# A 3x3x2 scheme with 15 half products in place of pairs with 11, in the second layer of an attention and two-layer kernel

## The chip, the cores and the metric

The kernel runs on one core of one Trainium2 chip. A core has TensorE (products into PSUM), VectorE (DVE), ScalarE (ACT) and GpSimd (POOL), each with its own instruction stream in program order, and queues for transfers, of which this kernel uses SyncE's (SP). PSUM has eight banks of 128 partitions by 512 f32 columns. The metric is the device time of one execution in microseconds; less is better.

## The reference

Decayed linear attention on 4 x 8 heads of 768 steps, then two layers of two products each on 3072 rows. Only the second layer is touched by the change.

```python
x = _moe_ref(attn_out)              # (3072, 384) -> (3072, 384), rational function between two products
...
def _moe2_ref(x, w_in, w_out) -> np.ndarray:
    h = x @ w_in                    # (3072, 384) @ (384, 2048)
    g = h * np.cos(h)
    return (g @ w_out).astype(np.float32)
```

## The kernel before

Everything is transposed: a layer takes x as 384 rows (three chunks of 128, `NK`) by 3072 columns, six blocks (`NC`) of 512 columns (`TB`), and goes over the 2048 inner rows in 16 steps (`NF`) of 128. One step of one block makes h (128 x 512) as a first product over the three chunks, then g = h cos h on ACT and DVE, then a second product of g into three accumulators in PSUM (`acc`, three banks). To keep f32 accuracy each operand is split into a high and a low part (`hi` rounded to f32r by ACT, `lo` = rest by POOL or DVE), and each product is three passes of TensorE (`PASSES`: hi hi, hi lo, lo hi). So a plain step has 9 matmuls of 512 columns for h and 9 for the second product.

From the second layer's third block on, steps go in pairs (`by_seven`, L486): two steps (two 128-row parts of w_in), two of the three chunks and two column halves of 256 make a 2x2x2 scheme with seven half products, and the third chunk is added plainly. A pair has 11 half products of three passes (`seven`, L573): 21 matmuls of 256 columns and 6 of 512, as both column halves of the third chunk share a weight. The sums of weights (`weights_sums0/1`, L500) and of x (`x_sums0/1`, L533) are made ahead, on DVE and POOL; the sums of products are made by ACT copies out of PSUM and POOL additions (`seven_out0/1`, `seven_sums`), and added into h's bank by DVE (`seven_add`, L624).

The order on each engine is written by hand (`manual_schedule`), step by step in `layers(n)` (L813): first product of step n (`gemm1`), ACT and DVE work of the steps before (`rational`, `cosine`), second product of the step 4 or 5 before (`lag`, `second`), then loads, splits and conversions of weights. The first layer has n from 0 to 95 (`N1` = 96), the second from 96 to 191; block 2 of the second begins at n = 128. Weights come as f64 words and are converted by ACT and DVE (`to_f32`, `tick`), split by `w_hi` and `w_lo`; those of the second layer's w_in go to DRAM (`wd`) and come back by `w_load`, those of w_out stay in SBUF (`ws[1]`, tiles `w1_0` to `w1_15`). Finished accumulators are copied out by `acc_out` (L668), the middle one by DVE, the other two by ACT.

h's banks in pairs: `h_bank` (L495) gives b1, b2, r1, b0 in turn; r0 takes the products that are copied out.

Of the kernel before, what the change touches and what calls it, by code (L numbers as in the profile page):

```python
# [19 lines left out]
HP = 4  # L20
# [19 lines left out]
def attn_then_two_moe(ctx, tc, kqT, aT, vP, w1i, w1o, ma, mb, w2i, w2o, out):  # L40
# [6 lines left out]
    wd = dram.tile([NF + NO, 128, 2, DM], F32, name="wd")  # L47
# [37 lines left out]
    in_p = main.enter_context(tc.tile_pool(name="in", bufs=3))  # L85
# [27 lines left out]
    ws = [[wp.tile([128, 2, DM], F32R, name=f"w{s}_{i}") for i in range(NF)] for s in range(2)]  # L113
# [38 lines left out]
    def words_bank(w):  # L152

        if slot[0] < LEAD:
            return words_t
        if N1 + 3 < slot[0] - LEAD < N1 + 2 * NF - 1:
            return bank(f"r{w[2] % 2}", (128, TB), I32)[:, :DM]
        return None
# [31 lines left out]
    def w_lo(engs):  # L190
        engs = list(engs)
        while to_lo:
            (m, s, i), hi = to_lo.pop(0)
            at = early(m, s, i)
            lo = ws[s][i][:, 1] if at is None else v_t[at % 3][:, :DM].bitcast(F32R)
            engs[0].tensor_tensor(
                out=lo, in0=stage.pop((m, s, i)), in1=hi.bitcast(F32), op=ALU.subtract
            )
            engs.append(engs.pop(0))
            ready.add((m, s, i))  # L200
            if at is not None:
                nc.sync.dma_start(out=wd[at, :, 0], in_=hi.bitcast(F32))
                nc.sync.dma_start(out=wd[at, :, 1], in_=lo.bitcast(F32))
# [254 lines left out]
    N1 = NC * NF  # L458
# [23 lines left out]
    s_in = {}  # L482
    x_t = {}
    held = {}

    def by_seven(n):  # L486

        m, blk, f = where(n)
        return m == 1 and 1 < blk and (blk < NC - 1 or f < NF - 2)

    def lag(n):

        return 5 if n < N1 or by_seven(n) else 4

    def h_bank(n):  # L495
        if n < N1 + 2 * NF:
            return bank(f"b{n % 3}")
        return bank((("b1", "b2"), ("r1", "b0"))[n % 2][n // 2 % 2])

    def weights_sums0(j):  # L500

        a = temp("z", shape=(128, 4, 128))
        for i in range(2):
            w = ws[0][2 * j + i].bitcast(F32)
            nc.vector.tensor_tensor(
                out=a[:, 2 * i:2 * i + 2].rearrange("p a b -> p (a b)"), in0=w[:, 0, 0:256], in1=w[:, 1, 0:256], op=ALU.add
            )
        held["sums"] = t = temp("g", shape=(128, 4, 128))
        nc.gpsimd.tensor_tensor(out=t[:, 0], in0=a[:, 2], in1=a[:, 3], op=ALU.add)
        nc.gpsimd.tensor_tensor(out=t[:, 1], in0=t[:, 0], in1=a[:, 0], op=ALU.subtract)  # L510
        nc.gpsimd.tensor_tensor(out=t[:, 2], in0=a[:, 0], in1=a[:, 2], op=ALU.subtract)
        nc.gpsimd.tensor_tensor(out=t[:, 3], in0=a[:, 1], in1=t[:, 1], op=ALU.subtract)

    def weights_sums1(j):

        if j == 0:
            held["kq"] = const.tile([128, 5 * 2 * HP * C], F32R, tag="kq", name="s_in")
            held["s1"] = [const.tile([128, 128], F32R, tag=f"s{i}", name=f"s1_{i}") for i in range(2)]
        if j < 6:
            flat = held["kq"][:, 2 * DM * j:2 * DM * (j + 1)].rearrange("p (a b c) -> p a b c", a=2, b=3)  # L520
            s = [flat[:, i] for i in range(2)]
        else:
            s = [
                const.tile([128, 3, 128], F32R, tag=f"v{2 * (j - 6) + i}", name=f"s_in{j}{i}") for i in range(2)
            ]
        first = held["s1"] if j == NF // 2 - 1 else [ws[0][2 * j + 1][:, i, 0:128] for i in range(2)]
        t = held.pop("sums")
        for hi, lo, of in ((first[0], first[1], t[:, 0]), (s[0], s[1], t[:, 1:])):
            nc.scalar.activation(out=hi, in_=of, func=AF.Copy)
            nc.gpsimd.tensor_tensor(out=lo, in0=of, in1=hi.bitcast(F32), op=ALU.subtract)  # L530
        s_in[j] = [[first[i]] + [s[i][:, k] for k in range(3)] for i in range(2)]

    def x_sums0(blk):  # L533

        raw = xt[1, blk][:, 1].bitcast(F32)
        t = [in_p.tile([128, TB], F32, tag="p", name="t") for _ in range(2)]
        nc.vector.tensor_tensor(
            out=t[0].rearrange("p (a b) -> p a b", a=2), in0=raw[:, 0:2, HT:],
            in1=raw[:, 0].rearrange("p (a b) -> p a b", a=2), op=ALU.subtract,
        )  # L540
        nc.vector.tensor_tensor(out=t[1][:, :HT], in0=raw[:, 1, HT:], in1=t[0][:, :HT], op=ALU.subtract)
        nc.vector.tensor_tensor(out=t[1][:, HT:], in0=raw[:, 1, :HT], in1=t[1][:, :HT], op=ALU.subtract)
        held["t"] = t

    def x_sums1(blk):

        t = held.pop("t")
        tag, words = (("st", 4 * DM), ("a", 3 * HP * (C + 1)))[blk % 2]
        to = const.tile([128, words], F32R, tag=tag, name=f"x_t{blk}")[:, :6 * HT].rearrange(
            "p (a b c) -> p a b c", a=2, b=3  # L550
        )
        if blk < NC - 1:
            first = [xt[1, blk][:, i, 0, HT:] for i in range(2)]
        else:
            first = [held["kq"][:, 12 * DM + HT * i:12 * DM + HT * (i + 1)] for i in range(2)]
        x_t[blk] = [[first[i]] + [to[:, i, k] for k in range(3)] for i in range(2)]
        for hi, lo, of in (
            (first[0], first[1], t[0][:, :HT]), (to[:, 0, 0], to[:, 1, 0], t[0][:, HT:]),
            (to[:, 0, 1:], to[:, 1, 1:], t[1].rearrange("p (a b) -> p a b", a=2)),
        ):  # L560
            nc.scalar.activation(out=hi, in_=of, func=AF.Copy)
            nc.vector.tensor_tensor(out=lo, in0=of, in1=hi.bitcast(F32), op=ALU.subtract)

    def products(out, parts):

        left = sum(len(p) for p in parts)
        first = True
        for a, b, cs in parts:
            for w, xx in PASSES:
                nc.tensor.matmul(out[:, cs], a[w], b[xx], start=first, stop=True, skip_group_check=True)  # L570
                first = False

    def seven(n, which):  # L573

        _, blk, f = where(n)
        j = f // 2
        x, t, s = xt[1, blk], x_t[blk], s_in[j]
        e, o = ([[ws[0][2 * j + i][:, w, k * 128:(k + 1) * 128] for w in range(2)] for k in range(NK)] for i in range(2))
        left, right, both = slice(0, HT), slice(HT, TB), slice(0, TB)

        def part(k, cs):
            return [x[:, i, k, cs] for i in range(2)]

        def sums(of, k):
            return [of[i][k] for i in range(2)]

        if which == 0:
            y = bank("r0")
            products(y, ((sums(s, 1), sums(t, 2), left), (e[0], part(0, left), right)))
            T[n] = {"m": y}  # L590
        elif which == 1:
            y = bank("r0")
            products(y, ((sums(s, 0), sums(t, 0), left), (sums(s, 2), sums(t, 1), right)))
            T[n]["m"] = y
        else:
            he, ho = h_bank(n - 1), h_bank(n)
            products(he, ((e[2], part(2, both), both), (e[1], part(1, left), left), (sums(s, 3), part(1, right), right)))
            products(ho, ((o[2], part(2, both), both), (o[1], sums(t, 3), left)))
            T[n - 1]["h"] = he
            T[n] = {"h": ho, "of": T[n - 1]}  # L600

    def seven_out0(n):

        d = T[n]
        d["q"] = raw_p.tile([128, 3, HT], F32, tag="raw", name="q")
        nc.scalar.activation(out=d["q"][:, 0:2].rearrange("p a b -> p (a b)"), in_=d["m"], func=AF.Copy)
        nc.gpsimd.tensor_tensor(out=d["q"][:, 0], in0=d["q"][:, 0], in1=d["q"][:, 1], op=ALU.add)

    def seven_out1(n):
        d = T[n]  # L610
        d["p"] = temp("z", shape=(128, 2, HT))
        nc.scalar.activation(out=d["p"].rearrange("p a b -> p (a b)"), in_=d["m"], func=AF.Copy)

    def seven_sums(n):

        d = T[n]
        q, p = d["q"], d["p"]
        nc.gpsimd.tensor_tensor(out=q[:, 2], in0=q[:, 0], in1=p[:, 0], op=ALU.add)
        d["o"] = temp("g", shape=(128, 2, HT))
        nc.gpsimd.tensor_tensor(  # L620
            out=d["o"], in0=q[:, 0:3:2], in1=p[:, 1:2].to_broadcast([128, 2, HT]), op=ALU.add
        )

    def seven_add(n):  # L624

        d = T[n]
# [496 lines left out]
```

## Time and profile before

| | us |
|---|---|
| three timed executions | 939.75, 944.48, 943.57 (median 943.57) |
| profiled execution | 940.65 |
| its span, first to last instruction | 938.8 |
| TensorE busy | 906.9 |
| DVE, ACT, POOL busy | 713.1, 688.8, 723.7 |
| first product by pairs, from its first matmul | 661.40 on |
| last matmul ends | 932.7 |

The profile names an instruction group by its line, engine, operation and tiles (out<-in). Busy matmul intervals overlap each other, since a matmul is recorded until its last result; how often one can begin is read from the starts of the next. The granted TensorE clock is full from the first layer on.

### The profile page before, as it was taken

The numbers are of one execution on the slowest core, as the hardware profiler recorded it, in microseconds if no ns is written. First come the engines' busy times: TensorE is split into PE (matmuls) and PEld (weight loads), VectorE is DVE, ScalarE is ACT, GpSimd is POOL, SyncE is SP. The second block draws the span as 40 slices with busy tenths as digits, with TensorE's granted clock in tenths as the row PEclk, the third lists the DMA queues.
The fourth block names the chain that finished last, engine by engine and source line by source line (L and its number), as shares of the span: only waits on it lengthen the run. The fifth ranks groups of instructions, "written<-read, shape, count | busy, mean of one in ns | idle before, by whom it ended". The sixth has DMA issues, their size and how long they took to land.

```text
span 938.8 us, 15168 instructions
## 1 busy us (share of the span) xinstructions
PE 906.9 (97%) x5255; PEld 746.8 (80%) x5255; DVE 713.1 (76%) x1172; ACT 688.8 (73%) x1261; POOL 723.7 (77%) x701
## 2 busy tenths in 40 slices
PE   7898899999999999999999999999899999999997
PEld 6676777878888888888888888888788888888885
DVE  8988969999999989979979846456457557467442
ACT  6899987978779878888778877665466656666663
POOL 5998999989889989889979755567676666666662
PEclk9899999999999999999999999999999999999999
DMA  8999941111113122132155242120010010100001
GB/s 283 293 312 324 305 150 31 34 35 35 67 68 102 34 85 84 51 118 68 35 184 174 96 152 84 52 68 1 1 68 1 16 53 1 68 1 1 35 1 37
DMA packets 47029, 84.66 MB, mean 90 GB/s; under 512 B 5505, under 2 KB 22145, under 8 KB 46945
## 3 DMA queue, kind: packets, MB, share of 16 engines
q1 hardware_dynamic: 46944, 83.62, 27.4%
q8 instruction: 43, 0.70, 0.3%
q14 instruction: 42, 0.34, 0.1%
HBM read 63.15 MB, written 20.45 MB: 89 GB/s over the span
## 4 chain that ended last, share of the span: by engine, by line
PE 80%; DVE 6%; ACT 5%; DMA 4%; issue 2%; POOL 2%; SPq 1%; DVEq 0%; ACTq 0%
PE acc L660 40%; PE b L644 26%; PE r L570 6%; PE b L570 6%; DMA x0d<-g 1%; DVE p L253 1%; DMA x<-x0d 1%; DMA spare<-w1i 1%; DVE st L72 1%; DMA spare<-w1o 1%; DVE g L726 1%; ACT g L719 1%; DMA kq<-kqT 1%; DVE g L713 0%; DVE ah L277 0%
## 5 line engine op out<-in xcount | busy, mean ns | idle before, releaser
L660 PE MATMUL acc<-hi,w 128*128 128x512 f32 x1152 | 392.3, 395 | 0.0
L695 POOL TENSOR_TENSOR lo<-g,hi 128x512 fp32r<-128x512 f32 x192 | 257.3, 1340 | 111.9 <-ACT hi L690 105.4
L644 PE MATMUL b<-x,w 128*128 128x512 f32 x1170 | 294.5, 396 | 0.6 <-DVE g L713 0.5
L644 PEld LDWEIGHTS b<-x,w 128*128 128x128 f32 x1170 | 219.2, 188 | 54.8 <-DVE g L713 2.1
L660 PEld LDWEIGHTS acc<-hi,w 128*128 128x128 f32 x1152 | 216.5, 188 | 49.5
L660 PE MATMUL acc<-lo,w 128*128 128x512 f32 x576 | 227.4, 395 | 0.0
L690 ACT ACTIVATE hi<-g 128x512 fp32r<-128x512 f32 x192 | 121.2, 631 | 106.7 <-DVE g L726 51.8
L721 POOL TENSOR_TENSOR z<-z,ah 128x512 f32<-128x512 f32 x96 | 127.2, 1325 | 8.0
L660 PEld LDWEIGHTS acc<-lo,w 128*128 128x128 f32 x576 | 108.2, 188 | 23.2
L748 DVE TENSOR_TENSOR g<-ah,b 128x512 f32<-128x512 f32 x80 | 54.6, 682 | 77.3 <-ACT ah L746 77.3
L79 DVE SCALAR_TENSOR_TENSOR ah<-z,b 128x512 f32<-128x512 int32 x80 | 54.7, 684 | 44.0 <-ACT z L78 43.5
L722 DVE TENSOR_TENSOR g<-g,b 128x512 f32<-128x512 f32 x96 | 65.3, 681 | 24.9 <-ACT g L719 24.3
L720 POOL TENSOR_SCALAR z<-ah,cq 128x512 f32<-128x512 f32 x96 | 75.0, 781 | 1.1 <-ACT ah L718 0.9
L719 ACT ACTIVATE g<-b,cq 128x512 f32<-128x512 f32 x96 | 74.5, 776 | 0.0
L726 DVE SCALAR_TENSOR_TENSOR g<-g,cq,r 128x512 f32<-128x512 f32 x96 | 70.9, 739 | 0.1
L713 DVE SCALAR_TENSOR_TENSOR g<-g,cq,b 128x512 f32<-128x512 f32 x96 | 70.7, 736 | 0.0
L746 ACT ACTIVATE ah<-ah,half_pi 128x512 f32<-128x512 f32 x96 | 68.6, 716 | 0.0
L730 ACT ACTIVATE r<-z,lnb 128x512 f32<-128x512 f32 x96 | 66.6, 694 | 1.8 <-POOL z L721 1.7
L715 DVE SCALAR_TENSOR_TENSOR r<-z,r 128x512 f32<-128x512 f32 x96 | 65.6, 684 | 0.0
L710 DVE SCALAR_TENSOR_TENSOR z<-z,r 128x512 f32<-128x512 f32 x96 | 65.0, 677 | 0.0
L718 ACT ACTIVATE ah<-b 128x512 f32<-128x512 f32 x96 | 56.4, 588 | 7.4 <-PE b L644 6.8
L731 ACT ACTIVATE r<-r 128x512 f32<-128x512 f32 x96 | 55.9, 582 | 3.1
(154 smaller groups left out, 1493.4 us busy)
## 6 DMA issues: line engine op xcount, KB each, us to landing
kq<-kqT SPq DMA_DIRECT2D x24, 512.0 KB, 5.5
raw<-w2i SPq DMA_DIRECT2D x16, 384.0 KB, 3.1
w<-wd SPq DMA_DIRECT2D x16, 384.0 KB, 3.1
raw<-w2o SPq DMA_DIRECT2D x16, 384.0 KB, 3.0
v<-vP SPq DMA_DIRECT2D x24, 192.0 KB, 5.4
x<-x0d SPq DMA_DIRECT2D x18, 256.0 KB, 3.4
x1d<-o SPq DMA_DIRECT2D x18, 256.0 KB, 2.1
x<-x1d SPq DMA_DIRECT2D x18, 256.0 KB, 3.6
```

The lines of the kernel that those rows point to most:

```text
L570: nc.tensor.matmul(out[:, cs], a[w], b[xx], start=first, stop=True, skip_group_check=True)
L644: nc.tensor.matmul(h, ws[0][f][:, w, ks], x[:, xx, kk, :], start=i == 0, stop=i == 8)
L660: nc.tensor.matmul(acc[k], ws[1][f][:, w, ks], d[g], start=first and i == 0, stop=last and i == 2)
L690: nc.scalar.activation(out=t["hi"], in_=t["g"], func=AF.Copy)
L695: eng.tensor_tensor(out=t["lo"], in0=t["g"], in1=t["hi"].bitcast(F32), op=ALU.subtract)
L713: nc.vector.scalar_tensor_tensor(g, g, cq[:, 3:4], two["h"], ALU.add, ALU.mult)
L719: nc.scalar.activation(out=g, in_=h, func=AF.Identity, scale=cq[:, 5:6], bias=cq[:, 4:5])
L720: nc.gpsimd.tensor_scalar(zz, ah, cq[:, 1:2], cq[:, 0:1], ALU.mult, ALU.add)
L721: nc.gpsimd.tensor_tensor(out=zz, in0=zz, in1=ah, op=ALU.mult)
L726: nc.vector.scalar_tensor_tensor(g, g, cq[:, 2:3], r, ALU.add, ALU.mult)
L730: nc.scalar.activation(out=r, in_=two["z"], func=AF.Ln, scale=LN_S, bias=lnb)
L746: nc.scalar.activation(out=t["r"], in_=t["r"], func=AF.Sin, bias=half_pi)
```

## The change

From the third block of the second layer on, three steps go together (`threes(k)`, 64 slots and five more for what is left). Three 128-row parts of w_in, three chunks and two column halves make a 3x3x2 scheme with 15 half products ("0" to "14") where a plain group has 18. A group takes two PSUM banks f0 and f2 (in turn b0, r0 and b1, r1) and b2 for f1. Products add into halves of these banks; between them ACT copies a half or a bank to SBUF (`s5`, `s63`, `t21`, `t`), DVE adds a copy onto a half in PSUM, and TensorE adds further products onto the sum. The 16th step of a block is a plain one (kind 3).

The sums of weights (11 DVE and 6 POOL additions of 128 columns per group, `w_prepare`) and of x (nine DVE additions of 256 columns and one of 512 per block, `x_prepare`) are generators that give out a few operations per slot; from block 1 of the second layer on `prepare` runs them, later `threes` does (`prepare_dve(n)`, `prepare_act(n)`, `prepare_pool(n)`: so many units of each engine at that place in the order). The sums use the unsplit f32 weights, stored to a new DRAM tile `wf` by `w_lo` in the first layer. They take the place of w_out's tiles in SBUF, so w_out's split parts are stored to `wd` and loaded again, 384 KB a step, one step ahead of the cosine and three ahead of the second product. Pairs and all that belongs to them go. `in_p` gets four buffers for three; the second layer's output copies use `z` and `g` buffers.

```diff
+    N3 = NF // 3
...
             ready.add((m, s, i))
+            if m == 1 and s == 1:
+                nc.sync.dma_start(out=wd[NF + i], in_=ws[1][i].bitcast(F32))
             if at is not None:
+                nc.sync.dma_start(out=wf[i], in_=full)
...
+    def first_product(t, blk, name, tile, half, start=False):
...
+        w, x = wa[t][wk], xb[blk][xk]
+        for i, (p, q) in enumerate(PASSES):
+            nc.tensor.matmul(
+                tile[:, half], w[p], x[q], start=start and i == 0, stop=True, skip_group_check=True
+            )
...
+    def level0(n, t, blk):
+        d = three_of[n] = {"f0": bank(f"b{n % 2}"), "f2": bank(f"r{n % 2}")}
+        first_product(t, blk, "5", d["f0"], RIGHT, True)
+        first_product(t, blk, "6", d["f2"], LEFT, True)
+        first_product(t, blk, "3", d["f2"], RIGHT)
...
+        if k + 1 in cons:
+            c = cons[k + 1]
+            c["w"] = wp.tile([128, 2, DM], F32R, tag=f"w1_{12 + c['at'] % 4}", name="w_out")
+            nc.sync.dma_start(out=c["w"].bitcast(F32), in_=wd[NF + c["f"]])
+        c, p = cons.get(k), cons.get(k - 1)
...
+        elif k - 2 in cons:
+            g2 = second_product(cons[k - 2])
...
+        z()
+        more = []
+        if kind == 0:
+            angle()
+            if d is None:
+                level0(n, t, blk)
+                d = three_of[n]
+            f0, f2 = d["f0"], d["f2"]
+            parts_g()
+            copy(q["s5"], f0[:, RIGHT])
+            copy(q["s63"], f2)
+            g2(5)
+            first_product(t, blk, "10", f0, RIGHT)
+            first_product(t, blk, "13", f2, LEFT)
+            copy(q["t21"], f0[:, RIGHT], -1.0)
+            prepare_dve(8)
+            nc.vector.tensor_tensor(out=f2[:, RIGHT], in0=q["t21"], in1=f2[:, LEFT], op=ALU.add)
+            sine()
+            more = prepare_act(1)
+            times()
+            g2(4)
+        elif kind == 1:
+            f0, f2 = d["f0"], d["f2"]
+            first_product(t, blk, "0", f0, RIGHT)
+            first_product(t, blk, "14", f2, LEFT)
+            d["f1"] = f1 = bank("b2")
+            nc.vector.tensor_tensor(out=f1[:, RIGHT], in0=f0[:, RIGHT], in1=q["s63"][:, LEFT], op=ALU.subtract)
+            copy(q["t"], f2[:, LEFT])
+            parts_g()
+            angle()
+            g2(5)
+            first_product(t, blk, "8", f0, RIGHT)
+            first_product(t, blk, "9", f2, LEFT)
+            prepare_dve(5)
+            nc.vector.tensor_tensor(out=f1[:, LEFT], in0=f0[:, RIGHT], in1=q["s63"][:, RIGHT], op=ALU.add)
+            nc.vector.tensor_tensor(out=q["u"], in0=q["s63"][:, RIGHT], in1=f2[:, LEFT], op=ALU.subtract)
+            nc.vector.tensor_tensor(out=f2[:, LEFT], in0=f2[:, LEFT], in1=q["s5"], op=ALU.subtract)
+            sine()
+            more = prepare_act(2)
+            times()
+            g2(4)
+        elif kind == 2:
+            f0, f1, f2 = d["f0"], d["f1"], d["f2"]
+            angle()
+            first_product(t, blk, "4", f0, RIGHT)
+            nc.vector.tensor_tensor(out=f0[:, LEFT], in0=f0[:, RIGHT], in1=q["u"], op=ALU.add)
+            nc.vector.tensor_tensor(out=f0[:, RIGHT], in0=f0[:, RIGHT], in1=q["t"], op=ALU.subtract)
+            parts_g()
+            sine()
+            more = prepare_act(3)
+            prepare_dve(7)
+            times()
+            g2(5)
+            first_product(t, blk, "12", f2, LEFT)
+            first_product(t, blk, "7", f2, RIGHT)
+            first_product(t, blk, "11", f1, LEFT)
+            first_product(t, blk, "2", f1, RIGHT)
+            first_product(t, blk, "1", f0, RIGHT)
+            g2(4)
...
+        else:
+            angle()
+            parts_g()
+            sine()
+            times()
+            more = prepare_act(2)
+            prepare_dve(4)
+            g2(9)
+            if active:
+                if blk + 1 < NC:
+                    level0(n, 0, blk + 1)
+                h = bank("b2")
...
+        prepare_pool(3)
+        to_rest.extend(more)
+        acc_out()
...
-        for n in range(NU + 1 - LEAD, 2 * N1 + 4):
+        for n in range(NU + 1 - LEAD, F0):
             layers(n)
+        for k in range(SLOTS):
+            threes(k)
         acc_out()
```

Here `z`, `angle`, `sine`, `times` and `parts_g` are the cosine's operations: ACT's integer quotient, DVE's reduced angle, ACT's sine, DVE's product g, and for the step before ACT's high and POOL's low part of g. `g2(n)` issues the next n of a step's nine second products. `F0` = 128 is the first n of block 2.

## Rows read from the trace of the kernel before

**Rows 1.** The page's part 1: busy time, share of the span, instructions.

```profile
PE 906.9 (97%) x5255; PEld 746.8 (80%) x5255; DVE 713.1 (76%) x1172; ACT 688.8 (73%) x1261; POOL 723.7 (77%) x701
```

**Rows 2.** Stretches: length, busy us (instructions) of PE, PEld, DVE, ACT, POOL, clock, DMA.

```profile
594.20:661.40 67.20, 67.20 (x290) 54.14 (x288) 38.74 (x60) 38.62 (x74) 44.99 (x57) 1.00 0.09 30
661.40:684.00 22.60, 18.77 (x107) 16.11 (x106) 9.06 (x14) 11.72 (x23) 16.09 (x22) 1.00 0.14 46
684.00:913.60 229.60, 229.60 (x1282) 199.04 (x1281) 139.68 (x204) 143.03 (x254) 154.31 (x144) 1.00 0.06 21
```

**Rows 3.** The chain that ended last, in order: start, us, engine, tile, line, instructions.

```profile
691.50 2.46 PE b L570 x15
...
704.11 0.71 PE r L570 x6
704.82 2.09 PE acc L660 x9
...
707.62 2.46 PE b L570 x15
...
920.09 12.61 PE acc L660 x54
```

**Rows 4.** Who waited for whom, TensorE from 661: us in total, times, longest.

```profile
PE b L570 <- DVE g L748: 2.8, 1, 2.8
...
PE r L570 <- ACT q L606: 1.1, 1, 1.1
```

**Rows 5.** Timeline: start, us, engine, line, operation, tiles, count, idle before and releaser.

```profile
667.81 1.32 PE L570 MATMUL b<-x,w 128*128 128x512 f32 x6 [2.76 <-DVE g L748]
...
744.75 0.40 PE L570 MATMUL r<-x,w 128*128 128x256 f32 x2
...
745.19 0.60 ACT L606 ACTIVATE q<-r 128x512 f32<-128x512 f32 x1 [1.88 <-PE r L570]
...
909.07 1.22 PE L570 MATMUL b<-x,w 128*128 128x512 f32 x6
```

**Rows 6.** Groups of ACT from 640 on: forms, count, busy us, mean ns, idle before.

```profile
L746 ACT ACTIVATE ah<-ah,half_pi 128x512 f32<-128x512 f32 x70 | 50.1, 718 | 0.0
L690 ACT ACTIVATE hi<-g 128x512 fp32r<-128x512 f32 x71 | 45.0, 634 | 28.7 <-DVE g L748 17.9 <-PE acc L660 10.8
...
L606 ACT ACTIVATE q<-r 128x512 f32<-128x512 f32 x31 | 18.5, 596 | 48.0 <-PE r L570 48.0
...
L561 ACT ACTIVATE x_t<-t 128x256 fp32r<-128x256 f32 x4 | 1.6, 406 | 0.0
```

**Rows 7.** The same groups for DVE.

```profile
L748 DVE TENSOR_TENSOR g<-ah,b 128x512 f32<-128x512 f32 x54 | 36.8, 682 | 57.4 <-ACT ah L746 57.4
...
L629 DVE TENSOR_TENSOR b<-b,q 128x512 f32<-128x512 f32 x31 | 21.4, 692 | 1.8 <-PE b L570 1.8
```

**Rows 8.** Timeline of DVE, then of POOL, at the sums of x for a block.

```profile
771.10 1.79 DVE L537 TENSOR_TENSOR t<-x 128x512 f32<-128x512 f32 x1
772.92 0.43 DVE L541 TENSOR_TENSOR t<-x,t 128x256 f32<-128x256 f32 x1
773.38 0.85 DVE L542 TENSOR_TENSOR t<-x,t 128x256 f32<-128x256 f32 x1
774.15 0.67 DVE L748 TENSOR_TENSOR g<-ah,b 128x512 f32<-128x512 f32 x1
774.75 0.68 DVE L79 SCALAR_TENSOR_TENSOR ah<-z,r 128x512 f32<-128x512 int32 x1
...
771.06 1.28 POOL L695 TENSOR_TENSOR lo<-g,hi 128x512 fp32r<-128x512 f32 x1 [0.28 <-ACT hi L690]
773.01 0.94 POOL L618 TENSOR_TENSOR q<-q,z 128x256 f32<-128x256 f32 x1 [0.67 <-ACT z L612]
```

**Rows 9.** Groups of POOL from 640 on.

```profile
L695 POOL TENSOR_TENSOR lo<-g,hi 128x512 fp32r<-128x512 f32 x71 | 91.9, 1294 | 33.1 <-ACT hi L690 33.1
```

**Rows 10.** Transfers: issues by tile, count, KB each, median us to landing.

```profile
w<-wd SPq DMA_DIRECT2D x16, 384.0 KB, 3.1
```

## What was predicted before the change was run

> **What bounds it now.** I read the busy shares first: TensorE is busy for 97% of the span, the others for 73 to 77% [rows 1]. Then the stretches: from 594.20 to 661.40 (second block of the second layer) TensorE has no idle time at all, from 661.40 to 684.00 it is busy for 18.77 of 22.60 us, and from 684.00 to 913.60 again for all of it [rows 2]. The change works from 661.40 on, so what counts is TensorE's own time there, and the 22.60 - 18.77 = 3.8 us that it stands at the first pairs; two waits make these up, 2.8 us for DVE's product with the cosine and 1.1 us for ACT's copy of a product [rows 4]. The other engines have room there (DVE 139.68, ACT 143.03, POOL 154.31 of 229.60 us [rows 2]), so only a wait that TensorE meets can cost.
>
> **Prices on TensorE.** The chain gives them: nine full products (512 columns) take 2.09 to 2.10 us, 54 take 12.61, so F = 0.2335 us; six half products (256 columns) take 0.71 us, and fifteen of which six are full 2.46, so h = (2.46 - 6 x 0.2335)/9 = 0.1177 us [rows 3]. A pair has 21 h and 6 F for its first product and 18 F for its second: 8.08 us; two pairs lie from 691.50 to 707.62, 16.12 us, 8.06 each [rows 3]. A half product costs hardly more than half of a full one, so to count columns is right. The Trainium skill (TensorE: Matmul & The Clock Gate, "Back-to-back issue gap") gives other spacings for streams of weight loads and products, 81 ns at 128 columns and 131 at 512; between them a half product would be near 98 ns, an estimate from that page, and the exchange counted below would cost 249 x 0.098 - 168 x 0.131 = 2.4 us. The rows show 118 and 233.5 ns and decide against it.
>
> **What is removed and added on TensorE.** Before: 31 pairs and two plain steps, 651 h and 204 F of first products (the code's count). After: 20 groups of 45 h (15 half products of three passes), one plain step of 9 F in each of four blocks: 900 h and 36 F. The difference is 249 x 0.1177 - 168 x 0.2335 = 29.3 - 39.2 = **-9.9 us**. The second products are the same 68 steps of 9 F. The two waits of the first pairs go with the pairs: **-3.8 us**; what is late in their place is in the next paragraphs. Together 13.7 us can be won; new waits are taken off.
>
> **The round trips in a group.** Each group goes six times from TensorE to ACT or DVE and back into the same PSUM half. I laid one group out, TensorE without a stop: 5, 6, 3 until 1.06 us, five second products until 2.23, 10 and 13 until 2.93, four second ones until 3.87; 0 and 14 until 4.57, five until 5.74, 8 and 9 until 6.45, four until 7.38; 4 until 7.73, five until 8.90, the last five until 10.67, four until 11.60. A result is ready 0.2 us after the next product could begin, and ACT begins 0.04 us later (744.75 + 0.40 to 745.19); back it takes 0.05 us [rows 5]. ACT's passes: sine 0.72, rounding 0.63, full copy (the integer z too) 0.60, half copy 0.41 from the nearest row [rows 6]. DVE's full operations with one input in PSUM take 0.68 to 0.69 [rows 7] and follow each other at 0.60 (774.15 to 774.75); a half one is put at 0.43 [rows 8], with 0.35 (half of 0.69) and 0.69 (no gain from the size) as bounds. Then the copy of 5 ends at 0.95, that of 6 and 3 at 1.9 (wanted at 2.2 and 2.6), the sum on 13 at 3.6 (wanted by 14 at 4.2), the one on 0 at 4.9 (wanted at 5.7), the one on 8 at 6.75 (wanted by 4 at 7.4), the last on 4 at 9.4 (wanted at 10.3). The tightest room is 0.6 us: **0 us** in a group that has nothing else to do, from 0 to 0.8 per group if a half sum costs 0.69 and each handover a little more. The low parts on POOL, 1.29 us each [rows 9], come at 7.0 for a second product at 7.96. Of 11.60 us ACT has some 6.3 and DVE 6.2, so both keep up.
>
> **Sums from SBUF (the preparation).** These are DVE additions with both inputs in SBUF. Without POOL's lo one of 256 columns takes 0.43 us, beside POOL's additions 0.85, and one of 512 columns 1.79 [rows 8]; of 128 columns I take 0.3 to 0.6 as an estimate from these. Where the time of such an operation is doubled, POOL is at work in the same microsecond (771.06, 773.01). The Trainium skill says so too (SBUF — State Buffer, "Who interferes with whom": a DVE instruction with two SBUF inputs contends with a GpSimd instruction that reads SBUF, one with at most one does not); the rows agree, since the sums out of PSUM keep 0.69 us beside a busy POOL. With every such addition doubled, as the rule would have it at a POOL that is never idle, the two blocks below would lose 6 us, with none doubled 2.5. In block 1 this work lies beside full steps of 4.2 us whose cosine has more than a step of room, with DVE at 38.74 and POOL at 44.99 of 67.20 us [rows 2], part of them the pairs' own sums: 0 us, up to 2 if POOL runs late. In block 2 (rest of the weights, x of block 3) I count 0.5 us. In blocks 3 and 4 the order that the generators give is: in slot 4 three additions of 256 columns ahead of the sum that product 4 awaits, in slot 5 three more and one of 512 ahead of the cosine's product, so ACT's rounding and behind it the copies of the next 5, 6, 3 come late. At the middle of both prices: product 4 waits 0.3, the second accumulator's bank (DVE's copy out of it stands behind the same work) 0.8, products 10 and 13 0.7; with 0.1 us at each stop for weights not loaded ahead (667.81: six products 1.32 against 1.22 [rows 5]) 2.2 us a block, **4.4 us** for both, bounds 0 (hidden altogether) and 6.
>
> **Start, block ends, tail.** Slot 4 of block 2 has no second products at all, as no cosine has begun before slot 3: products 8, 4 and the first low part are waited for, about 1.2 us, and slot 1 carries two old cosines, 0.4; with the reloads **1.9 us**, bounds 0.5 and 4. At each of three block ends the plain step's product is finished just when the next slot begins, and ACT has its z first and the copies of 5, 6, 3 behind it: z until 0.8, rounding until 1.35, copies until 1.7 and 2.2, with only five second products (1.17 us) as cover: 0.7 and two reloads, **2.7 us** for three, bounds 0 and 5. Block 5 has the bank's wait alone, **0.5**. At the end five steps of second products stand behind a chain of z, angle, sine, product, rounding, low part that runs at 2.2 us a step against 2.1: **0.8 us**, bounds 0 and 2.5. The reload of the second weights, 384 KB a step that land in 3.1 us [rows 10], is issued three steps ahead of its use; the stores of wd and wf follow DVE and POOL work that is long done on SP's queue: 0. The last copy and store stay.
>
> **The sum.** 0.5 + 4.4 + 1.9 + 2.7 + 0.5 + 0.8 = 10.8 us of new waits against 13.7: **-2.9 us**. The profiled execution takes 940.65 us (span 938.8), so it would take 937.8. The three timed ones lie at 939.75, 943.57 and 944.48; with the profiled one their mean is 942.1, and 942.1 - 2.9 = 939.2: the forecast for a typical execution is **939**. Against the median of the three, 943.57, that is 4.6 less, but only 2.9 of it is the change.
>
> **Rivals.** *The waits are covered* (faster): the sums from SBUF meet POOL seldom (0.43 us each), and the copies at the block ends lie earlier, so that 4 to 5 us of waits remain: 942.1 - 9 = 933. For it speaks that DVE and ACT have 40% room and that every trip inside a group had 0.6 us left; against it that the places where I find stops are places where the order of one queue, not its load, makes them. *The round trips don't fit* (slower): each group works in one f0 and one f2 half at a time, so TensorE cannot run ahead of ACT and DVE by more than one trip. From 0.15 us lost per group on (2.9/20) the gain is gone, and at 0.5 us a group, less than one half sum at 0.69 in place of 0.43 at two trips and one late handover, the kernel takes 939 + 10 = 949. For it speaks that six trips in 11.6 us are as many as the pair has in 16; against it the 0.6 us of room. *It doesn't do what it says*: with 45 half products in a row of other tiles h might be over 0.1177; at 0.1575 (39.2/249) nothing is saved on TensorE, and at 0.125 the gain shrinks by 900 x 0.0073 = 6.6 to a loss of 3.7: 946. Against it: in the pairs six halves with six weights take 0.71 wherever they stand.
>
> **How the numbers follow.** Forecast case (0 to 5 us gained, 937 to 942) 0.43; covered 0.38; round trips 0.14; dearer halves 0.05. Least waits (5 us) and most that the bounds give (18) make -8.7 to +4.3 about 942.1, and the runs' own spread adds 2: the range is 931 to 946; the likeliest case alone is 936 to 942.5. About 0.5% (4.7 us) is what a measurement of this kernel tells from no change. Faster by more: the covered case and a little of the forecast, 0.41; within: 0.44; slower: 0.15.
>
> **What would show it.** Right: from 661.40 to the last product some 268 us or a little under, TensorE's busy time there near 257; in the waits rows of first products against ACT's half copies at block starts and against DVE's f0, f1 sums in slots 4 and 5 of blocks 3 and 4; groups of 11.6 us without idle elsewhere. Wrong: idle time in every group (then the round trips decide), three half products at over 0.36 us (then the halves), stops in block 1 or in the first layer (then the preparation or the stores).

## The result: 0.7% slower, and where the profile after shows it

The changed kernel takes 949.47 us (median of nine runs, 946.19 to 952.0) against 943.41 for the kernel before (nine runs, 939.75 to 944.48): a ratio of 1.0069 [1.0051, 1.0087], 6.1 us slower. Forecast were 939 and a range of 931 to 946: the direction and the range were both wrong. The profiled execution took 949.87 us with a span of 948.2, 9.4 above the span before.

The page's part 1 of the kernel after, for [rows 1]:

```profile
PE 905.6 (96%) x5336; PEld 743.7 (78%) x5336; DVE 743.1 (78%) x1293; ACT 697.4 (74%) x1298; POOL 687.3 (72%) x649
```

DVE has 30 us more to do and POOL 36 us less; over the whole span no engine but TensorE is near its limit. The stretches of after, for [rows 2] (length, then busy us and instructions of PE, PEld, DVE, ACT, POOL, granted clock, DMA share, GB/s):

```profile
594.20:661.40 67.20, 65.47 (x277) 51.35 (x277) 48.26 (x79) 37.04 (x71) 44.49 (x49) 1.00 0.29 95
...
666.30:693.00 26.70, 23.35 (x141) 19.77 (x140) 18.01 (x37) 15.49 (x35) 17.92 (x21) 1.00 0.43 141
693.00:941.60 248.60, 241.19 (x1410) 207.00 (x1408) 155.49 (x292) 155.56 (x293) 120.68 (x102) 1.00 0.36 112
```

Before, TensorE had no idle time from 594.20 to 661.40 and from 684.00 to 913.60. Now it stands in each of the three. Who it waits for, from 600 on, for [rows 4] (us in total, times, longest):

```profile
PE b L934 <- DVE b L1070: 3.6, 5, 1.6
PE b L934 <- DVE g L1020: 2.7, 4, 0.8
PE b L504 <- DVE g L599: 1.7, 4, 0.6
PE b L934 <- ACT s L1029: 1.4, 4, 0.5
PE acc L969 <- DVE z L541: 1.0, 2, 0.5
PE b L934 <- DVE b L1062: 0.8, 1, 0.8
```

L1070 is the sum that has to read a half of f0 before product 4 adds into it, L599 and L1020 are the cosine's product, L541 the copy of an accumulator out of its bank, all on DVE. Idle time is not the whole price of a stop. Worked out from the starts in the timeline (distance between two starts, less the products between them at F and h), a stop costs about 0.26 us more than the idle that is listed, since the products behind it have no weights loaded ahead (the load for the product of 676.45 begins at 676.44) and the last ones before it are recorded until their last result. By that count, which is used from here on, TensorE loses 2.9 us in block 1 and 17.7 us between the first group (666.32) and the last product (941.6); before, it lost nothing in block 1 and 4.1 us behind it. That stretch is 275.3 us long after and 271.3 before (661.40 to 932.7): 4.0 us more, and 6.9 with block 1. Of the other 2.5 of the 9.4 us, 1.7 lies ahead of both: the first layer's first product starts at 116.1 before and at 117.8 after, and in the thirteen profiles of this study between 114.2 and 119.1, though twelve of the kernels are the same up to there. The last 0.8, of which 0.5 stands behind the last product, was not followed up.

| term | forecast | measured |
|---|---|---|
| products saved on TensorE | -9.9 | -9.6 (271.3 - 4.1 = 267.2 against 275.3 - 17.7 = 257.6) |
| waits of the first pairs | -3.8 | -4.1, gone |
| trips inside a plain group | 0 | 0 |
| three block ends | 2.7 | 2.2 |
| bank in block 5; tail | 0.5; 0.8 | 0.3; 1.0 |
| block 1 | 0 (up to 2) | 2.9 |
| start, with block 2's preparation | 1.9 + 0.5 | 7.0 |
| blocks 3 and 4 | 4.4 (0 to 6) | 7.1 |

The new waits come to 20.5 us where 10.8 were forecast; with 13.7 us won that is a loss of 6.8, near the 6.1 of the medians. (Slots are counted from 0 in each block.) The last three rows of the table hold the whole error. What stands there in DVE's order, at the start and in block 3 of the kernel after (timeline: start, us, engine, line, operation, tiles, count, idle before and releaser):

```profile
672.24 3.81 DVE L655 TENSOR_TENSOR w_f<-w_f 128x128 f32<-128x128 f32 x5
675.97 0.42 DVE L1070 TENSOR_TENSOR b<-b,s 128x256 f32<-128x256 f32 x1
...
676.45 0.63 PE L934 MATMUL b<-x,w_kq 128*128 128x256 f32 x3 [1.62 <-DVE b L1070]
...
680.92 0.89 DVE L655 TENSOR_TENSOR w_f<-w_f 128x128 f32<-128x128 f32 x4
...
751.89 1.41 DVE L655 TENSOR_TENSOR x_f<-x_f,x 128x256 f32<-128x256 f32 x1
753.22 0.41 DVE L655 TENSOR_TENSOR x_f<-x,x_f 128x256 f32<-128x256 f32 x1
753.55 0.42 DVE L1070 TENSOR_TENSOR b<-b,s 128x256 f32<-128x256 f32 x1
...
754.02 0.63 PE L934 MATMUL b<-x,w_kq 128*128 128x256 f32 x3 [0.63 <-DVE b L1070]
```

Five additions of 128 columns (L655, the preparation) take 3.81 us ahead of the sum that TensorE awaits, and four take 0.89 us at 680.92. In the first stretch POOL is at work without a pause, in the second it has nothing to do:

```profile
671.05 1.89 POOL L649 TENSOR_TENSOR w_kq<-w_f,w_kq 128x768 fp32r<-128x768 f32 x1
672.86 0.55 POOL L649 TENSOR_TENSOR w<-w_f,w 128x128 fp32r<-128x128 f32 x1
673.37 1.34 POOL L555 TENSOR_TENSOR lo<-g,hi 128x512 fp32r<-128x512 f32 x1
674.67 0.77 POOL L649 TENSOR_TENSOR w<-w_f,w 128x256 fp32r<-128x256 f32 x1
675.40 0.50 POOL L655 TENSOR_TENSOR w_f<-w_f 128x128 f32<-128x128 f32 x1
...
678.70 0.46 POOL L655 TENSOR_TENSOR w_f<-w_f,w_f 128x128 f32<-128x128 f32 x1
687.36 1.29 POOL L1026 TENSOR_TENSOR lo<-g,hi 128x512 fp32r<-128x512 f32 x1 [8.20 <-ACT hi L1025]
```

From 672.24 to 676.05 POOL ends five operations (672.94, 673.41, 674.71, 675.44, 675.90) and DVE does five additions, which in the records of the trace end at 673.09, 673.55, 674.86, 675.59 and 676.05: each 0.15 us behind the POOL operation beside it, whatever its own size.

The same records for all 55 of DVE's preparing additions of 128 columns say when this happens. Thirteen meet no operation of POOL and take 0.28 to 0.29 us; eight begin ahead of the POOL operation that they meet and take 0.28 to 0.29 us too; the other 34 begin behind one and end behind it (32 of them by 0.15 us), and take up to 1.40 us. With 256 columns 17 of 36 stay at 0.41 to 0.43 us, and the 19 that begin behind a POOL operation end 0.28 or 0.29 us behind it.

So the theory to be tested: the preparation's additions on DVE make the loss, by their place (ahead of what TensorE awaits) and by their length (beside POOL's reads). The rivals: other causes at the same places, that is the round trips, the order of ACT's copies at block starts, or the start's missing second products.

### The profile page after: what moved, and what is told of

It is laid out like the page before. It is cut to its first block, busy times and chain, and to the rows that moved or that the text cites. A ratio compares the mean times of both kernels' runs of the same rounds, so it can differ in the third digit from the quotient of the medians.

```text
span 948.2 us, 15697 instructions
## 1 busy us (share of the span) xinstructions
PE 905.6 (96%) x5336; PEld 743.7 (78%) x5336; DVE 743.1 (78%) x1293; ACT 697.4 (74%) x1298; POOL 687.3 (72%) x649
## 4 chain that ended last, share of the span: by engine, by line
PE 65%; DVE 14%; ACT 5%; POOL 5%; DMA 5%; issue 5%; SPq 0%; DVEq 0%; ACTq 0%; POOLq 0%
PE acc L520 22%; PE b L504 22%; PE acc L969 11%; PE b L934 5%; PE r L934 4%; DVE x_f L655 2%; DVE w_f L655 2%; POOL lo L555 1%; DMA a<-aT 1%; DVE p L256 1%; DMA spare<-w1o 1%; PE b L1114 1%; DVE st L73 1%; ACT hi L550 1%; DMA spare<-w1i 1%
## 5 line engine op out<-in xcount | busy, mean ns | idle before, releaser
L504 PE MATMUL b<-x,w 128*128 128x512 f32 x1143 | 288.2, 396 | 2.4 <-DVE g L599 1.7
L504 PEld LDWEIGHTS b<-x,w 128*128 128x128 f32 x1143 | 213.8, 188 | 56.7 <-DVE g L599 3.7
L520 PE MATMUL acc<-hi,w 128*128 128x512 f32 x744 | 254.4, 396 | 0.0
L520 PEld LDWEIGHTS acc<-hi,w 128*128 128x128 f32 x744 | 139.9, 188 | 34.4 <-DVE z L541 0.3
L550 ACT ACTIVATE hi<-g 128x512 fp32r<-128x512 f32 x128 | 80.7, 630 | 93.4 <-DVE g L586 51.9
L520 PE MATMUL acc<-lo,w 128*128 128x512 f32 x372 | 147.0, 395 | 0.0
L969 PE MATMUL acc<-hi,w_out 128*128 128x512 f32 x384 | 130.6, 396 | 1.1 <-DVE z L541 1.0
L520 PEld LDWEIGHTS acc<-lo,w 128*128 128x128 f32 x372 | 69.9, 188 | 16.7
L969 PEld LDWEIGHTS acc<-hi,w_out 128*128 128x128 f32 x384 | 68.4, 188 | 12.2 <-DVE z L541 2.4
L969 PE MATMUL acc<-lo,w_out 128*128 128x512 f32 x192 | 76.2, 397 | 0.6 <-POOL lo L1026 0.5
```

The source lines that it names most:

```text
L504: nc.tensor.matmul(h, ws[0][f][:, w, ks], x[:, xx, kk, :], start=i == 0, stop=i == 8)
L520: nc.tensor.matmul(acc[k], ws[1][f][:, w, ks], d[g], start=first and i == 0, stop=last and i == 2)
L550: nc.scalar.activation(out=t["hi"], in_=t["g"], func=AF.Copy)
L969: nc.tensor.matmul(acc[k], item["w"][:, w, ks], item[g], start=first, stop=last)
```

## The experiments

Each stands on the changed kernel. "Waits" is TensorE's lost time by the count above, in block 1 and from the first group on, in the profile of that kernel; ratios are to the kernel before, run on the same chip. In experiments 5, 6, 7 and 9 to 11 the count also holds some time in which TensorE did not stand but ran at a granted clock of 0.50 (2.4, 2.8 and some 3 us, then 1.4 to 1.5 us; last section).

| kernel | median us | ratio | waits, block 1 | waits after |
|---|---|---|---|---|
| the change | 949.47 | 1.0069 [1.0051, 1.0087] | 2.9 | 17.7 |
| 1 constants for DVE's additions | 935.43 | 0.9913 [0.9885, 0.9942] | 0 | 8.0 |
| 2 additions behind the sums | 944.02 | 1.0001 [0.9979, 1.0022] | 2.8 | 12.0 |
| 3 x on POOL | 941.56 | 0.9977 [0.9961, 0.9992] | 2.5 | 11.0 |
| 4 copies first | 947.85 | 1.0041 [1.0023, 1.006] | 2.5 | 15.6 |
| 5 all additions on POOL | 946.02 | 1.0036 [1.002, 1.0053] | 3.1 | 16.0 |
| 6 the same, copies first | 942.89 | 1.0007 [0.9984, 1.0031] | 3.1 | 13.4 |
| 7 the same, old products spread | 943.52 | 1.0004 [0.9985, 1.0023] | 3.1 | 13.8 |
| 8 constants on POOL | 938.81 | 0.9947 [0.9929, 0.9964] | 0 | 11.8 |
| 9 2, 3 and 4 together | 938.03 | 0.996 [0.9944, 0.9975] | 2.6 | 9.0 |
| 10 the same, 7 a step in block 1 | 937.42 | 0.9965 [0.9947, 0.9983] | 1.1 | 9.3 |
| 11 the same, old products spread | 936.37 | 0.9952 [0.9932, 0.9973] | 1.5 | 8.2 |

**1. The additions left out.**

```diff
-        (eng or nc.vector).tensor_tensor(out=out, in0=a, in1=b, op=op)
+        if eng is None:
+            nc.vector.memset(out, 0.5)
+        else:
+            eng.tensor_tensor(out=out, in0=a, in1=b, op=op)
```

> The changed kernel with each of DVE's preparing additions (weights and x) replaced by the writing of a constant of the same size at the same place; the sums are left out, so the output is not the reference's. Theory 'preparation' (the new waits beyond the forecast come from DVE additions with two SBUF inputs, lengthened by POOL's reads: 2.9 us in block 1, some 4 at the start of block 2, 3.6 each in blocks 3 and 4): about 12 us less than the changed kernel, near 937, and TensorE's waits from the first group on fall from 17.7 to 6 or 7 us. Theory 'round trips' (the chain product, copy, sum, product itself is too long): the waits stay, 2 us less at most.

Measured: 12.6 us of waits go (20.6 to 8.0), and the kernel is 0.9% faster than the one before. A constant of 128 columns takes 165 ns, one of 256 takes 272. Block 1 stands still nowhere:

```profile
594.20:661.40 67.20, 67.20 (x294) 54.39 (x293) 30.87 (x80) 41.77 (x79) 49.64 (x56) 1.00 0.25 84
```

So the preparation on DVE carries some 60% of the waits. Without it the rest of the change gains 8.2 us (0.87% of 943), near the 7.8 that the forecast's terms give with the preparation at 0 (2.9 + 0.5 + 4.4). What is left, 8.0 us, is the start (2.4), the block ends (2.1), the bank of block 5 and the tail (1.3) and some 1.8 in blocks 3 and 4.

**2. Their place.** In kinds 1 and 2 the additions go behind the slot's sums and the cosine's product:

```diff
-            prepare_dve(5)
             nc.vector.tensor_tensor(out=f1[:, LEFT], in0=f0[:, RIGHT], in1=q["s63"][:, RIGHT], op=ALU.add)
...
             times()
+            prepare_dve(5)
...
-            prepare_dve(7)
             times()
+            prepare_dve(7)
```

> The changed kernel with the preparing additions in the second and third slot of a group moved behind the slot's own sums and the cosine's product; all else as it is. Theory 'place' (it is only that they stand ahead of what TensorE waits for, whatever their length): some 8 to 9 us less, near 941, with block 1's 2.9 us left. Theory 'length' (DVE is late from the additions whatever their place): what is gained in one slot is lost in the next, 0 to 3 us less. 'Round trips': no change.

Measured: waits after fall by 5.7 us to 12.0, the time to that of the kernel before. In blocks 3 and 4 one stop is left where there were four:

```profile
750.74 0.50 PE L969 MATMUL acc<-hi,w_out 128*128 128x512 f32 x1 [1.20 <-DVE z L541]
```

The additions now stand ahead of the accumulator's copy, so each block loses 1.46 us instead of 3.57. The gain lies between what was expected of "place" alone (8 to 9 us) and of "length" (0 to 3): place is part of it, but moved additions find the next waiter.

**3. Off DVE, where POOL has room.** The additions of x for blocks 3 to 5 run on POOL.

```diff
-        (eng or nc.vector).tensor_tensor(out=out, in0=a, in1=b, op=op)
+        (eng or add_on[0]).tensor_tensor(out=out, in0=a, in1=b, op=op)
...
+        add_on[0] = nc.vector if blk == 2 else nc.gpsimd
```

> The changed kernel with the additions of x for blocks 3 to 5 on POOL in place of DVE (nine of 256 columns at 0.74 and one of 512 at 1.3 us a block). 'Preparation' in either form: the waits of slots 4 to 8 in blocks 3 and 4 go (7.1 us), POOL has 40% and more room there; some 6 us less, near 943.5. 'Round trips': no change; if POOL's order makes the low parts late, up to 3 us more.

Measured: 11.0 us of waits after; of the 3.57 us of blocks 3 and 4 only 0.32 each is left, and with this one edit the change is 0.2% faster than the kernel before. POOL had only 120.68 of 248.60 us to do there, and TensorE's waits for it stay at 0.5 us.

**4. ACT's order at block starts.** The copies of 5 and of 6, 3 go ahead of the integer quotient and the rounding.

```diff
+        early = kind == 0 and t == 0 and bi > 0
+        if early:
+            copy(q["s5"], d["f0"][:, RIGHT])
+            copy(q["s63"], d["f2"])
         z()
...
```

> The changed kernel with ACT's copies of products 5, 6 and 3 put ahead of the plain step's z and the rounding in the first slot of blocks 3, 4 and 5. If ACT's order there is the cause of the three waits of 0.7 us at product 10, 2 us less, near 947.5; if the products themselves come late, no change.

Measured: waits after fall by 2.1 us, and the three stops at block ends are gone. In the kernel after (ACT, then TensorE) the copy of 5 stands behind z and the rounding:

```profile
734.75 0.60 ACT L1007 ACTIVATE z<-b 128x512 int32<-128x512 f32 x1 [3.42 <-PE b L1114]
735.25 0.62 ACT L1025 ACTIVATE hi<-g 128x512 fp32r<-128x512 f32 x1
735.77 0.37 ACT L1029 ACTIVATE s<-b 128x256 f32<-128x256 f32 x1
...
736.19 0.62 PE L934 MATMUL b<-x_t,w 128*128 128x256 f32 x3 [0.31 <-ACT s L1029]
```

The mechanism of the block ends was right and its size nearly so (0.73 us each, 0.9 forecast).

**5. All preparing additions on POOL.**

```diff
-        (eng or nc.vector).tensor_tensor(out=out, in0=a, in1=b, op=op)
+        nc.gpsimd.tensor_tensor(out=out, in0=a, in1=b, op=op)
```

> The changed kernel with all preparing additions on POOL (weights and x), none on DVE. Theory 'port' (DVE's additions are long only because POOL reads SBUF at the same time; POOL has room for them): no wait in block 1, waits from the first group on some 7 us as with constants in place of the sums; near 937. Theory 'work' (the sums are too much beside the cosine on whichever engine): POOL becomes late in block 1 (some 17 us of additions more in 67 us, of which 45 were used), its low parts are waited for, and what DVE gains is lost: 944 or more.

Measured: 946.02 us, as theory "work" has it. DVE's waits are exchanged for POOL's:

```profile
PE acc L969 <- POOL lo L1026: 2.9, 3, 2.2
PE acc L969 <- POOL lo L555: 2.4, 1, 2.4
PE b L504 <- DVE g L599: 2.0, 2, 1.1
```

POOL is busy for 57.87 of 67.20 us in block 1 and for 54.72 of 58.60 us behind it, so the low parts of the cosine come late. In blocks 1 and 2 neither engine has the room to do all of it in time. This run holds DVE's additions away from POOL's reads and so does not settle by itself why they were long on DVE; experiment 8 does.

**6, 7. The same with the copies first, then with the last four second products of block 1 spread** (7, 7, 7, 7, 8 over five slots, so that the slots at the start have more to cover with).

```diff
-            g2 = second_product(item)
+            olds.append([9, second_product(item)])
...
```

> All preparing additions on POOL and ACT's copies first at the block starts: the two gains add, 2.2 us under the run with the additions alone on POOL, near 935; that is 0.9% under the kernel before. If the copies' gain hangs on DVE being late, no difference.

> The same, and block 1's last four second products spread over five slots (7, 7, 7, 7, 8 matmuls), so that slot 4 of block 2 has some. If slot 4's lack of cover makes the 2.2 us of waits there, 1 to 1.5 us less than without it, near 934; the copy out of the accumulators then stands a slot later and may take 0.5 back.

Measured: 942.89 and 943.52, where 935 and 934 were expected from a 937 that experiment 5 had not reached. The first takes 2.6 us off the waits, 2.1 of it the block ends; the second is inconclusive, since POOL's lateness lies over the slots that it was to help.

**8. POOL's reads taken away.** DVE's additions all stay; the preparation's low parts and additions on POOL become constants.

```diff
-            nc.gpsimd.tensor_tensor(out=lo, in0=of, in1=hi.bitcast(F32), op=ALU.subtract)
+            nc.gpsimd.memset(lo.bitcast(F32), 0.0)
...
+            eng.memset(out, 0.5)
```

> The changed kernel with POOL's part of the preparation (its additions and the low parts of the sums) replaced by constants of the same size at the same place, which read nothing from SBUF; DVE's additions all stay. The low parts of the sums are left out, so the output is not the reference's. Theory 'port': DVE's additions of 128 columns shorten from 0.65 us to near 0.3, block 1's 2.9 us go to under 1, and of the waits in blocks 3 and 4, where the cosine's low parts still run on POOL, a third; 5 to 7 us less, near 943. Theory 'number' (the additions are too many at their own length): no change.

Measured: DVE's instructions are the same, and they are shorter. The groups of DVE (forms, count, busy us, mean ns, idle before), of after and then of this kernel, and the five additions at the start:

```profile
L655 DVE TENSOR_TENSOR w_f<-w_f 128x128 f32<-128x128 f32 x50 | 29.7, 649 | 5.2 <-DMA w_f<-wf 5.2
```

```profile
L656 DVE TENSOR_TENSOR w_f<-w_f 128x128 f32<-128x128 f32 x50 | 18.6, 427 | 5.0 <-DMA w_f<-wf 5.0
...
669.80 2.20 DVE L656 TENSOR_TENSOR w_f<-w_f 128x128 f32<-128x128 f32 x5
```

Block 1 has no stop, and waits after are 11.8 us against 17.7. That DVE's additions are drawn out by POOL's operations is thereby shown, and not only argued from their standing side by side. POOL's constants are also shorter than what they replace, so the mean alone does not tell reading from mere work; the single records do: 13 additions of 128 columns stand beside nothing but a constant that POOL writes and take 0.28 to 0.29 us, as the 27 that meet nothing, while the 7 that begin behind one of the cosine's low parts end 0.15 us behind it (1.31 us on the mean). In blocks 3 and 4, where POOL still computes these low parts, 2.5 us a block remain: of the 3.57 there the 1.05 of slot 8 is POOL's preparation, the rest is the additions' place and the low parts beside them.

**9 to 11. Put together.** First edits 2, 3 and 4; then block 1 gives out 7 units a step and not 9 (an addition of a weight is one unit, one of x two); then the spread of 7 as well.

```diff
-            prepare_dve(9)
+            prepare_dve(7)
```

> The changed kernel with x's additions for blocks 3 to 5 on POOL, the copies first at the block starts, and the weights' additions behind the slot's own work. If these gains lie in different places they add: of the 17.7 us of waits from the first group on, 7.1 less 0.9 in blocks 3 and 4, 2.2 at the block starts and some 1.5 at the start of block 2 go; about 10 us less than the changed kernel, 939.5, 0.4 to 0.5% under the kernel before. If they overlap, 942.

> The same with 7 in place of 9 units of preparation per slot in block 1. If block 1's waits come from too many lengthened additions in one slot, their 2.9 us fall to 1 or less: near 937.5. If DVE meets POOL there at any rate, no change, or the work moved into block 2 costs what is gained.

> The same, with block 1's last four second products spread over five slots, so that slot 4 of block 2 has cover for its trips. If the lack of cover makes the 2.2 us of waits there, 1 to 1.5 us less than without; if the round trips there are late for another reason, no change.

Measured: 938.03, 937.42 and 936.37; by their intervals the three can't be told apart. The smaller portions take block 1's waits from 2.6 to 1.1 us, but at the start of block 2 one stop grows from 0.40 us of idle to 1.80. No more additions come there than in experiment 9; the same five come at another moment of POOL's order and take longer (DVE, experiment 9, then 10):

```profile
671.92 2.62 DVE L655 TENSOR_TENSOR w_f<-w_f 128x128 f32<-128x128 f32 x5
```

```profile
668.85 4.02 DVE L655 TENSOR_TENSOR w_f<-w_f 128x128 f32<-128x128 f32 x5
```

Which operation of POOL an addition meets is thus decided by the order far ahead of it. With the spread the stops of slot 4 (2.2 us in the kernel after, a product or a low part of the block's first cosine each time) are gone but for 0.4 us, and the large one stays, in the last kernel 2.45 us of idle (DVE, then TensorE):

```profile
669.68 4.18 DVE L655 TENSOR_TENSOR w_f<-w_f 128x128 f32<-128x128 f32 x5
...
674.80 0.62 PE L936 MATMUL b<-x_t,w_kq 128*128 128x256 f32 x3 [2.45 <-DVE b L1101]
```

Since edit 2 the five additions stand behind their slot's own sums, and so ahead of the two sums on product 4 in the next slot, of which L1101 is the second; product 1 goes into the half that it works on, and waits. The last kernel takes 0.9952 [0.9932, 0.9973] of the time of the kernel before. Its start alone still holds 5.1 us of lost time, 1.5 of it at the lower clock; the preparation for the first two groups has to be done in a stretch in which DVE and POOL are both loaded.

## Why the prediction was wrong, step by step

**TensorE's own terms were right.** Half products cost what they were taken at: three start 0.35 to 0.36 us apart in the chain of after, for [rows 3] (start, us, engine, tile, line, instructions), and a plain group of block 3 lasts from 772.53 to 784.23, 11.70 us where 11.60 were laid out:

```profile
772.53 0.59 PE b L934 x3
773.13 0.72 PE r L934 x6
773.84 1.17 PE acc L969 x5
775.02 0.35 PE b L934 x3
775.37 0.36 PE r L934 x3
775.72 0.94 PE acc L969 x4
```

The surplus of 0.1 is the stop at its beginning. Two rivals fall with that: there is no "dearer half", and the "round trips" do fit, with no idle time in any group that has nothing else to do. That rival gave 949, and the kernel took 949.5; the agreement is chance, since its mechanism isn't there.

**Block ends, block 5 and tail** were right in place and nearly in size (table). For the block ends experiment 4 shows the cause, ACT's copies standing where the prediction put them; block 5's bank and the tail were not tested alone.

**The failed step is the price of the sums from SBUF.** For 128 columns 0.3 to 0.6 us were taken "as an estimate from these", that is from operations of 256 and 512 columns at which doubling was seen [rows 8]. What was seen there was no factor of two but the remainder of a POOL operation that had begun before: POOL's of 773.01 ends at 773.95, and DVE's of 773.38 at 774.23, 0.28 us behind it [rows 8]. The addition of 128 columns alone takes 0.28 us (627.83), the mean of fifty is 0.65, and four in block 1 (656.92) take 4.43, 1.11 each. At 256 columns the range is 0.41 to 1.96; the longest (645.15) stands beside a POOL operation of 2.03 us. A short operation is thus lengthened by more than a long one, in proportion, and the preparation consists of short ones. The Trainium skill, cited in the prediction for this (SBUF — State Buffer, "Who interferes with whom"), says that the clash is with a GpSimd instruction that reads SBUF and not with one that only writes it; experiment 8 bears that out, 649 against 427 ns on the mean and 0.28 to 0.29 us beside constants alone. The page states the clash and no doubling: the factor of two was the prediction's own, where the rows show a wait for the end of POOL's operation.

**Three terms fell with it.** Block 1 was put at 0, because the cosine had "more than a step of room" and DVE 38.74 of 67.20 us. DVE's load did stay below the limit, 48.26 of 67.20 us now, but the portion of one step did not fit: five additions of 3.85 us stand between two products of the cosine, and one step is 4.2 us:

```profile
634.65 0.68 DVE L80 SCALAR_TENSOR_TENSOR ah<-z,b 128x512 f32<-128x512 int32 x1
635.25 3.85 DVE L655 TENSOR_TENSOR w_f<-w_f 128x128 f32<-128x128 f32 x5
639.03 0.68 DVE L599 TENSOR_TENSOR g<-ah,b 128x512 f32<-128x512 f32 x1
...
639.76 2.37 PE L504 MATMUL b<-x,w 128*128 128x512 f32 x9 [0.50 <-DVE g L599]
```

Four such steps make 2.9 us; in experiments 1 and 8 they are gone. The prediction had named stops in block 1 as a sign that the preparation was wrong. At the start block 2's preparation was put at 0.5 us; the stop at 676.45 alone is 1.9 (idle and reload). The slot without second products was seen and under-sized: 2.2 us where about 1.2 were meant. In blocks 3 and 4 slots 4 and 5 stop as was foretold, but for longer, and slot 8 was left out: its two additions of 256 columns take 2.43 us beside POOL's own parts and hold back the cosine's product, for which the group of 772.53 waits (1.04 us a block).

```profile
769.36 2.43 DVE L655 TENSOR_TENSOR x_f<-x 128x256 f32<-128x256 f32 x2
771.71 0.67 DVE L1020 TENSOR_TENSOR g<-ah,b 128x512 f32<-128x512 f32 x1
772.53 0.59 PE L934 MATMUL b<-x_t,w_v 128*128 128x256 f32 x3 [0.80 <-DVE g L1020]
```

**The chances.** The sign of the change hung on the preparation: it was 5 of 10.8 us of new waits in the sum and 12.6 of 20.6 on the chip. The upper bounds that the prediction itself named (6 for blocks 3 and 4, 2 for block 1, 4 for the start) add up, with 0.5 for block 2 and 4.0 for block ends, bank and tail, to 16.5 us, a loss of 2.8; and 7.1, 2.9 and 7.0 lie beyond each of them, since the first was a bound on a factor of two and the other two had no price of a long addition in them. The range was also cut short in its own terms. The 18 us of its upper end are 6, 4, 5, 0.5 and 2.5, without the 2 of block 1 and the 0.5 of block 2, and 942.1 + 4.3 + 2 is 948.4 and not 946; with all that it named the end is 950.9 (942.1 + 20.5 - 13.7 + 2). That would have taken in the measured 949.47, but by luck: the width would have come from terms other than the one that failed. A fourth rival, "an addition waits for the POOL operation that it meets", would have pointed to a loss: fifty additions at 0.65 and not 0.45 are 10 us more on DVE, an estimate, much of it ahead of a waiting product.

## What to carry to other kernels

In this kernel a DVE addition with both operands in SBUF is priced by the POOL operation that may have begun before it (up to 1.40 us at 128 columns, 0.28 alone), not by its own size; many short ones in a row are the worst case. Work that fills idle time of an engine is placed behind what the bounding engine awaits, in portions shorter than that slack, and on the engine that is idle in that very stage: one such move (x on POOL from block 3 on) turned 0.7% slower into 0.2% faster. Moving all of it to one engine only moves the lateness.

## What the runs showed of the hardware that was not expected

TensorE's clock fell in some kernels behind stops, and each fall cost more than some of the stops themselves. In experiment 6 a wait of 2.37 us ends at 667.48, and TensorE then runs without idle time at a granted clock of 0.50, 1.2 of 2.4 GHz (stretches: length, PE busy, clock, DMA share, GB/s):

```profile
668.40:669.40 1.00, 1.00 (x4) 0.50 0.00 0
...
671.40:672.40 1.00, 1.00 (x9) 1.00 0.00 0
```

Three half products take 0.64 us there (669.35 to 669.99) against 0.36, and the fall costs 1.4 us. Experiment 5 has the same wait, and behind it the clock stays at 1.00 (the product at its end, experiment 6, then 5; the stretch behind it in 5):

```profile
667.48 0.79 PE L969 MATMUL acc<-lo,w 128*128 128x512 f32 x1 [2.37 <-POOL lo L555]
```

```profile
668.19 0.50 PE L969 MATMUL acc<-lo,w 128*128 128x512 f32 x1 [2.37 <-POOL lo L555]
...
668.40:669.40 1.00, 1.00 (x6) 1.00 0.00 0
```

Falls are also seen behind the stop of 2.45 us in experiment 11, where the products from 675.9 to 678.8 lose another 1.45 us, behind one of 1.80 us in experiment 10, a second time in experiment 6 behind one of 1.04 us that ends at 688.08, and in experiment 9 behind three stops of 0.80, 0.17 and 0.24 us in a row (0.50 from 685 to 688). The wait of 2.76 us of the kernel before [rows 5], the one of 1.62 us of the kernel after and its own three stops in a row (0.79, 0.17 and 0.25 us, up to 688.71) were followed by a clock of 1.00. So neither the length of the last wait nor a few short ones in a row tell whether the clock falls; what else does was not tried.
